# Odd token classes of the backward transforms as 256-point products, with the remaining rotation on VectorE and ScalarE, and x1's gradient added in a DMA

## The chip, the cores and the metric

One core of a Trainium2 chip runs the whole program in one launch. The metric is the device time of one execution in microseconds (us). The kernel before took 1410.86 us (median of 3 runs, 1408.94 to 1412.46).

## What is computed

A transformer-like block and its gradients. x is 2048 tokens by 1024 channels, F = 3584 hidden channels, all in bf16. Forward: a layer norm, scaled and shifted by rows made from `silu(c) @ w_mod`; a spectral filter; a second layer norm; a two-layer perceptron.

```python
X = rfft2(x); X = X * (w_r + 1j * w_i); y = irfft2(X)
...
h = _layernorm(x) * (1 + ca) + sa
x = x + ga * _A_ref(h, A_w_r, A_w_i)
h = _layernorm(x) * (1 + cb) + sb
x = x + gb * _B_ref(h, B_w1, B_b1, B_w2, B_b2)
```

The outputs are this result and its gradients with respect to x, the filter (w_r, w_i), both weights and biases of the perceptron, c and w_mod.

## The kernel before

The transforms are written as matrix products with cosine and sine matrices. Each input is first folded along channels and along tokens into sums and differences, which sorts the frequencies into four classes: CE and SE (cosine and sine at even token frequencies) and CO and SO (odd ones). Of the even classes a product needs only two of four blocks of 128 folded tokens for each output half; of the odd classes it needs all four.

`spectral_core` holds the stages, once forward (`fwd` true) and once for the backward pass. `s_fwd` transforms tokens of one class: eight blocks `c8` of 128 channels, each into one accumulator of 512 columns, by two products of 256 columns a half for an even class and four of 512 for an odd one (L531, L538); an evacuation copies it into `U`. Eight `pair` steps follow: a channel transform (L577), evacuation by ScalarE (L781), the product with the filter and the filter's gradient on VectorE, and the result in `R`. `beside_bwd` puts four fills and some steps of w_mod's gradient (`rows34`) beside each pair. After pair 5, `s_inv` transforms CE and SE back (L647), after pair 7 `s_inv_half` does CO and SO (L663), in the backward pass in two halves of 256 columns each. `V` then goes through the channel inverse (`po`, L749) into four chunks of tokens.

`consume_bwd` treats each chunk on VectorE: unfold (`unfold_d`, `unfold_tok`), a product (`tt(tmp, o4, n1, ALU.mult)`; every `tt` shows as L194) whose column sum on TensorE is `accCA` (`halves_sum`), the layer norm's backward (`ln_bwd`), the gradient of x1 loaded from `d_gx1` by the SP queue into the buffer `n1` and added, and the store: one plain DMA on SP and two indirect ones on POOL.

TensorE's other work is a list of pieces of 16 products (`pieces`): gradients of w2 (`gw2_product`), which need transposed tiles of hh, and then of w1 (`gw1acc`), whose results go through a ring of eight tiles to POOL's queue. `fill(n)` takes the next n of them, and the calls of `fill` by hand set where they stand between the stages. The pieces that are left run at the end.

Before the transforms, a loop over four blocks `b` of 512 tokens runs the perceptron's backward product (`pg_pass`, L1105), the two layer norms' backward on VectorE, and the fold of the block before (`fold_quarter` into `fbuf2`); column sums go to `acc3`. The `turn` there is a transposing copy and not part of the change.

Each engine runs its queue in order. The order is made when the program is built: a planner goes by the order in the program, a few raised priorities (`tc.high_priority`), explicit edges (`issue_after`, `behind`), and estimated costs and due times, so an instruction that it holds ready can stand ahead of one that comes earlier in the program. `nc.any` copies go to VectorE or ScalarE, as it chooses.

## Time and profile before

| | |
|---|---|
| median of 3 runs | 1410.86 us (1408.94 to 1412.46) |
| profiled execution | 1412.42 us |
| its span, first to last instruction | 1410.6 us |
| TensorE (PE) busy | 1374.2 us, 97% |
| VectorE (DVE) busy | 1072.4 us, 76% |
| ScalarE (ACT) busy | 739.2 us, 52% |
| GpSimd (POOL) busy | 351.2 us, 25% |
| mean granted TensorE clock | 0.992 |

A timeline row gives the start and the length in us from the span's start, the engine, the line, the operation, what it writes and reads with shapes, and how many instructions were merged; the bracket at its end is the idle time before it and who ended it. A group's row gives its count, busy time and mean ns of one. Matmuls are pipelined, so one lasts longer than the distance to the next: costs are read from start to start.

### The profile page before, as it was taken

The page shows a single profiled execution, that of the slowest core. Times are in us where ns is not written, and L with a number is a line of the kernel's source. Part 1 is how long each engine was busy: PE and PEld are TensorE (multiplying, and loading weights), DVE is VectorE, ACT ScalarE, POOL GpSimd, SP SyncE. Part 2 cuts the span into 40 slices and gives each one's busy share as a digit, 9 for nine tenths or more (in the row PEclk, how much of TensorE's full clock was granted, in tenths as well). Part 3 has the DMA queues.
Part 4 walks back from the last instruction along what each step waited for, and adds up shares of the span by engine and source line. Part 5 has one row for each costly group of instructions (what it writes and reads, how often), then busy time and mean ns, then how long its engine had stood idle before and what let it go on. Part 6 is the DMA issues. An engine that isn't in the chain of part 4 may idle for free. (4 is left out here: it accounts for less than half of the span.)

```text
span 1410.6 us, 18696 instructions
## 1 busy us (share of the span) xinstructions
PE 1374.2 (97%) x6963; PEld 664.5 (47%) x6963; DVE 1072.4 (76%) x1507; ACT 739.2 (52%) x1059; POOL 351.2 (25%) x436
## 2 busy tenths in 40 slices
PE   5998999999999999999999999999999999999999
PEld 2545565444444444444444444444544565444444
DVE  5897889987978777887620688999498757979960
ACT  4774667667877765665314583243622444434311
POOL 5510623201112122112210010112345330322341
PEclk8899999999999999999999999999999999999999
DMA  9972666899787777696999499996689996897971
GB/s 330 301 234 57 176 165 200 265 283 350 256 258 242 229 242 249 189 287 224 298 271 232 138 237 321 259 259 209 197 265 288 261 253 173 218 250 189 286 270 38
DMA packets 361265, 333.22 MB, mean 236 GB/s; under 512 B 208026, under 2 KB 303152, under 8 KB 361046
## 3 DMA queue, kind: packets, MB, share of 16 engines
q1 hardware_dynamic: 319990, 206.01, 55.9%
q0 software_dynamic: 35424, 120.78, 24.5%
q10 hardware_dynamic: 5760, 5.25, 1.2%
q8 instruction: 54, 0.88, 0.3%
q14 instruction: 37, 0.30, 0.1%
HBM read 166.77 MB, written 115.92 MB: 200 GB/s over the span
## 5 line engine op out<-in xcount | busy, mean ns | idle before, releaser
L1105 PE MATMUL pg<-w1T,gzr 128*128 128x512 bf16 x896 | 196.0, 379 | 2.8 <-ACT gn3b L1121 2.8
L814 PE MATMUL pp<-gBoT,wt 128*128 128x512 bf16 x896 | 197.9, 380 | 0.8 <-DVE phr L820 0.4
L1464 PE MATMUL gw1acc<-gzh,n3n 128*128 128x512 bf16 x640 | 140.0, 379 | 0.2 <-DVE gwo L1468 0.2
L1105 PEld LDWEIGHTS <-gzr 128*128 128x128 bf16 x896 | 86.6, 98 | 111.1 <-issue 8.5
L1464 PEld LDWEIGHTS <-n3n 128*128 128x128 bf16 x896 | 87.3, 98 | 107.1 <-issue 3.3
L951 PEld LDWEIGHTS <-w 128*128 128x128 bf16 x896 | 87.2, 98 | 107.0 <-issue 2.5
L814 PEld LDWEIGHTS <-wt 128*128 128x128 bf16 x896 | 87.5, 98 | 104.0 <-issue 1.5
L951 PE MATMUL pz<-n3Tb,w 128*128 128x512 bf16 x448 | 99.2, 379 | 1.0 <-DVE w2sD L1027 1.0
L951 PE MATMUL pz<-n3Ta,w 128*128 128x512 bf16 x448 | 98.7, 379 | 0.0
L1005 PEld LDWEIGHTS <-hhA 128*128 128x128 bf16 x608 | 59.0, 98 | 73.1 <-issue 2.8
L1239 PE MATMUL gw2acc<-gB,hhsA 128*128 128x512 bf16 x416 | 92.2, 379 | 0.0
L954 ACT ACTIVATE gt<-pz,b_col 128x512 bf16<-128x512 f32 x112 | 72.8, 683 | 33.2 <-PE pz L951 33.0
L962 ACT ACTIVATE gt<-gt 128x2048 bf16<-128x2048 bf16 x28 | 53.5, 1911 | 64.8 <-DVE gt L194 64.8
L194 DVE TENSOR_TENSOR gt<-gt,gt 128x2048 bf16<-128x2048 bf16 x56 | 68.6, 1224 | 19.8 <-ACT gt L964 18.5
L194 DVE TENSOR_TENSOR ct<-ct 128x2048 bf16<-128x2048 bf16 x68 | 80.6, 1218 | 0.9
L1468 ACT CAST gwo<-gw1acc 128x512 bf16<-128x512 f32 x50 | 28.4, 581 | 89.3 <-PE gw1acc L1464 78.5
L1247 ACT CAST gwo<-gw2acc 128x512 bf16<-128x512 f32 x40 | 23.3, 584 | 93.6 <-PE gw2acc L1239 90.5
L1239 PEld LDWEIGHTS <-hhsA 128*128 128x128 bf16 x416 | 40.7, 98 | 47.4
L1470 POOL DMA_DIRECT2D out_dram<-gwo x53 | 29.2, 554 | 129.8 <-DVE gwo L1468 67.6
L1464 PE MATMUL gw1acc<-gzu,n3n 128*128 128x512 bf16 x256 | 55.6, 379 | 1.2 <-ACT gwo L1468 1.2
L958 ACT ACTIVATE gt<-gt 128x2048 bf16<-128x2048 bf16 x28 | 53.5, 1909 | 2.1 <-DVE hhC L194 1.3
L964 ACT ACTIVATE gt<-gt 128x2048 bf16<-128x2048 bf16 x28 | 53.4, 1907 | 0.4
(347 smaller groups left out, 2558.4 us busy)
## 6 DMA issues: line engine op xcount, KB each, us to landing
gzr<-d_gz SPq DMA_DIRECT2D x28, 512.0 KB
wblk<-in_w_mod_dram SPq DMA_DIRECT2D x12, 1024.0 KB
out_dram<-otl POOLq DMA_DIRECT2D x48, 256.0 KB, 4.9
d_ph<-pho POOLq DMA_DIRECT2D x21, 512.0 KB, 6.0
d_hh<-hhA POOLq DMA_DIRECT2D x19, 512.0 KB, 5.1
w<-in_B_w_dram SPq DMA_DIRECT2D x7, 1024.0 KB
hhC<-d_ph SPq DMA_DIRECT2D x14, 512.0 KB
w2sA<-d_ph SPq DMA_DIRECT2D x14, 512.0 KB
```

The lines of the kernel that those rows point to most:

```text
L194: return nc.vector.tensor_tensor(out=out, in0=a, in1=b, op=op)
L814: last_pe[0] = nc.tensor.matmul(pp[:], lhsT=wt[:, fc % 4, cch, :], rhs=gBoT[j][:, cch, :], start=(cch == 0), stop=(cch == NDC - 1))
L951: last_pe[0] = nc.tensor.matmul(pz[:], lhsT=w1s[g][:, cch, k * P:(k + 1) * P], rhs=n3T[:, cch, :], start=(cch == 0), stop=(cch == NDC - 1))
L954: z_in = nc.scalar.activation(out=zb[:, k, :], in_=pz[:], func=ACT.Identity, bias=b1_col[:, fc:fc + 1], scale=1.0)
L958: nc.scalar.activation(out=av, in_=zb, func=ACT.Square)
L962: nc.scalar.activation(out=sg, in_=bv, func=ACT.Sigmoid, scale=2.0 * GK)
L964: nc.scalar.activation(out=bv, in_=bv, func=ACT.Sigmoid, scale=-2.0 * GK)
L1005: last_pe[0] = nc.tensor.matmul(pbs[i][:], lhsT=hh[:, k, i * P:(i + 1) * P], rhs=wp[:, k, :], start=False, stop=(g == 6 and k == 3))
L1105: last_pg[0] = nc.tensor.matmul(pgs[i][:], lhsT=gzs[b, g][:, k, i * P:(i + 1) * P], rhs=w1Ts[g][:, k, h * KH:(h + 1) * KH], start=(g == 0 ...
L1239: nc.tensor.matmul(acc[:], lhsT=hh_of(fc)[:, t, :], rhs=gBs[t // 4][:, t % 4, h * KH:(h + 1) * KH], start=(t == 0), stop=(t == NT - 1))
L1464: nc.tensor.matmul(acc[:], lhsT=n3ns[t // 4][:, t % 4, cch * P:(cch + 1) * P], rhs=gz2[t // 8][:, t % 8, :], start=(t == 0), stop=(t == NT ...
L1470: eng.dma_start(out=out_4[cch * P:(cch + 1) * P, fg * 512:(fg + 1) * 512], in_=ob)
```

## The change

The four blocks of an odd class come in two couples of mirrored rows. Each couple is rotated by an angle that depends only on the row (`al`: its sine, cosine, tangent, and two of them negated; one number per partition), in the form a + t b and b - t a, with the cosine moved into the matrix. After that an odd class needs products with 256 columns only, two of two blocks for each output half; the two halves `ab` are evacuated, and their sum and difference, written to every second column, are the class.

- `turn_tokens` rotates the folded tokens: for each couple four scalings by ScalarE and two sums by VectorE, for couple 0 in the loop at `b == 2`, for couple 1 after the last fold. `turn_R` does the same to `R` before the inverse, for couple 0 after pair 5 and for couple 1 after pair 7.
- `half_class` takes the place of `s_fwd` and of `s_inv_half` for CO and SO in the backward pass. `make_fm` builds its matrix from the small matrix `em2` by VectorE, after the ten fills ahead of the transforms; the load of `em2` moves ahead of them.
- The odd matrices are no longer stored to `d_SF` and loaded again.
- The scratch of `turn_R` and the evacuation buffer `ab` lie in the same part of `smbf`.
- The gradient of x1 is added to the chunk by an accumulating DMA from POOL's queue, in place of the SP load and a VectorE addition.
- Fills move: one ahead of each of CO and SO and two less beside pair 0; one between CO's and SO's inverse; 3, 7, 7, 8 instead of 4, 7, 6, 8 in the chunks, and one instead of two after the third chunk's column sum.

```diff
@@ spectral_core
         for cl in (CE, SE, CO, SO):
-            Us[cl] = s_fwd(cl, fb, sms[cl % 2][:, cl // 2], evac_u)
+            if fwd or cl % 2 == 0:
+                Us[cl] = s_fwd(cl, fb, sms[cl % 2][:, cl // 2], evac_u)
+            else:
+                Us[cl] = reg.tile([P, 8, 512], BF16, name=f"U{cl}", tag=f"uv{cl}")
+                fill(1)
+                half_class(cl, Us[cl], lambda c8, i, cl=cl: fb[:, i, cl, c8 * P:(c8 + 1) * P], evac_u)
...
+                if not fwd and par == 1 and m % 2 == 1:
+                    turn_R(R, m // 2)
                 beside(par * 4 + m, r_in[0])
...
         for cl in (CO, SO):
-            for hf in range(1 if fwd else 2):
-                s_inv_half(cl, smis[1], hf)
+            if fwd:
+                s_inv_half(cl, smis[1], 0)
+                continue
...
+            half_class(cl, Vs[cl], r_cols, evac_v)
+            if cl == CO:
+                fill(1)
@@ token rotation
+    def turn_pair(a, b, r, cls, t1, t2):
+        for k, cl in enumerate(cls):
+            neg, pos = (3, 2) if cl == CO else (2, 3)
+            nc.scalar.activation(out=t1[:, k], in_=b[:, k], func=ACT.Identity, scale=al[:, neg, r:r + 1])
+            nc.scalar.activation(out=t2[:, k], in_=a[:, k], func=ACT.Identity, scale=al[:, pos, r:r + 1])
+        tt(a, a, t1, ALU.add)
+        return tt(b, b, t2, ALU.add)
...
             fold_quarter(b - 1, pru, gn3s[(b - 1) % 2][:])
+            if b == 2:
+                turn_tokens(0, gn3s[1][:])
...
             fold_quarter(b, ftmp, n3u[:])
+            fold2_in[b] = turn_tokens(1, n3u[:])
@@ matrix, products, rotation of R
+    def make_fm():
+        for r in range(2):
+            cos, ncos = al[:, 1, r:r + 1], al[:, 4, r:r + 1]
+            for k in range(2):
...
+    def half_class(cl, dst, lhs, evac):
+        k = cl // 2
+        for c0 in range(0, 8, 2):
+            k0 = c0 % 4
+            for c8 in range(c0, c0 + 2):
+                pu = (ps_f if c8 % 2 else ps_s)("pu")
+                for t in range(2):
+                    cols = slice(t * 256, (t + 1) * 256)
+                    for r in range(2):
+                        last_pu[0] = nc.tensor.matmul(pu[:, cols], lhsT=lhs(c8, 2 * r + (t + k) % 2), rhs=fm[:, r, k, t, :],
+                                                      start=(r == 0), stop=(r == 1))
+                with tc.high_priority():
+                    evac(ab[:, k0 + c8 - c0].rearrange("p t w -> p (t w)"), pu[:])
+            dv = dst[:, c0:c0 + 2, :].rearrange("p c (j e) -> p c j e", e=2)
+            for e, op in ((0, ALU.add), (1, ALU.subtract)):
+                tt(dv[:, :, :, e], ab[:, k0:k0 + 2, k, :], ab[:, k0:k0 + 2, 1 - k, :], op)
+
+    def turn_R(R, r):
+        t1, t2 = (smbf[:, 2048 + k * 2 * PW:2048 + (k + 1) * 2 * PW]...[:, :, :, 0:DF] for k in range(2))
+        for cl in (CO, SO):
+            turn_pair(R[:, cl * 4 + 2 * r:cl * 4 + 2 * r + 1, :, 0:DF], R[:, cl * 4 + 2 * r + 1:cl * 4 + 2 * r + 2, :, 0:DF],
+                      r, (cl,), t1, t2)
@@ consume_bwd
-        nc.sync.dma_start(out=n1, in_=chunk_rows(d_gx1, i))
-        tt(o4, o4, n1, ALU.add)
+        nc.gpsimd.dma_start(out=o4, in_=chunk_rows(d_gx1, i), accum_op=ALU.add)
         store_tok(out_1, o4, i)
-        fill((4, 7, 6, 8)[i])
+        fill((3, 7, 7, 8)[i])
         halves_sum(accCA[0], tmp, i == 0, i == 3)
-        fill(2)
+        fill(1 if i == 2 else 2)
@@ ahead of the transforms
-    for cl in (CE, SE, CO, SO):
-        nc.sync.dma_start(out=(smA2, smB2)[cl % 2][:, cl // 2], in_=d_SF[:, cl, 0:4 if cl % 2 else 2])
+    for cl in (CE, SE):
+        nc.sync.dma_start(out=smA2[:, cl // 2], in_=d_SF[:, cl])
     sums3(3, gn3s[1], pru)
+    nc.sync.dma_start(out=em2, in_=d_E[:, 0])
     fill(10)
-    nc.sync.dma_start(out=em2, in_=d_E[:, 0])
+    make_fm()
@@ beside_bwd
         for k in range(4):
-            fill(1)
+            fill(1 if n > 0 or k > 1 else 0)
```

More of the change, by code (lines that the diff above doesn't have):

```diff
@@ L104 @@
     gb_col = const.tile([P, NDC], FP32, name="gb_col")
+    al = const.tile([P, 5, 2], FP32, name="al")
     d_x1 = dram.tile([S, D], BF16, name="d_x1")
@@ L1128, with turn_tokens @@
     nc.vector.tensor_copy(out=u_rt[:], in_=u_bfc[:])
+    tt(al[:, 1, :], al[:, 1, :], al[:, 1, :], ALU.mult)
+    nc.vector.tensor_scalar(out=al[:, 1, :], in0=al[:, 1, :], scalar1=-2.0, scalar2=1.0, op0=ALU.mult, op1=ALU.add)
+    nc.vector.reciprocal(out=al[:, 3, :], in_=al[:, 1, :])
+    tt(al[:, 2, :], al[:, 0, :], al[:, 3, :], ALU.mult)
+    nc.vector.tensor_scalar(out=al[:, 3:5, :], in0=al[:, 2:0:-1, :], scalar1=-1.0, scalar2=None, op0=ALU.mult)
+    def turn_pair(a, b, r, cls, t1, t2):
[5 more added lines that the diff above has]
+        return tt(b, b, t2, ALU.add)
+    def turn_tokens(r, tmp):
+        return turn_pair(fbuf2[:, 2 * r, 1:4:2, :], fbuf2[:, 2 * r + 1, 1:4:2, :], r, (CO, SO), tmp[:, 0:2, :], tmp[:, 2:4, :])
     def gmod_steps(r, wrs, gws, gr):
@@ new lines, in half_class @@
+    def half_class(cl, dst, lhs, evac):
[4 more added lines that the diff above has]
+                pu = (ps_f if c8 % 2 else ps_s)("pu")
+                for t in range(2):
+                    cols = slice(t * 256, (t + 1) * 256)
[7 more added lines that the diff above has]
+                tt(dv[:, :, :, e], ab[:, k0:k0 + 2, k, :], ab[:, k0:k0 + 2, 1 - k, :], op)
@@ L1356 @@
+    def turn_R(R, r):
+        t1, t2 = (smbf[:, 2048 + k * 2 * PW:2048 + (k + 1) * 2 * PW].rearrange("p (o x w) -> p o x w", o=1, x=2)[:, :, :, 0:DF] for k in range(2))
+        for cl in (CO, SO):
+            turn_pair(R[:, cl * 4 + 2 * r:cl * 4 + 2 * r + 1, :, 0:DF], R[:, cl * 4 + 2 * r + 1:cl * 4 + 2 * r + 2, :, 0:DF],
+                      r, (cl,), t1, t2)
     empf = reg.tile([P, 2048 + 4 * PW], BF16, name="empf", tag="wt")
```

23 lines of the change are left out of this document (19 added, 4 removed).

## The prediction

> **What bounds the kernel now.** I read the busy shares first, then TensorE's waits from 850 us on, then TensorE's timeline through the backward transforms, then the timelines of VectorE and ScalarE beside it.
>
> The page's busy shares, the list of waits and the end of TensorE's timeline (start, length, line, operation, idle before):
>
> ```profile
> PE 1374.2 (97%) x6963; PEld 664.5 (47%) x6963; DVE 1072.4 (76%) x1507; ACT 739.2 (52%) x1059; POOL 351.2 (25%) x436
> PE pg L1105 <- ACT gn3b L1121: 2.8, 1, 2.8
> PE accCA L217 <- DVE ct L194: 1.6, 1, 1.6
> PE gw1acc L1464 <- ACT gwo L1468: 1.2, 1, 1.2
> ```
>
> ```profile
> 1327.47 51.96 PE L1464 MATMUL gw1acc<-gzu,n3n 128*128 128x512 bf16 x240 [1.20 <-ACT gwo L1468]
> 1379.27 27.79 PE L1464 MATMUL gw1acc<-gzh,n3n 128*128 128x512 bf16 x128
> ```
>
> TensorE is busy for 97% of the span and ends it: the last 80 us are its own product stream. From 850 us on it waits for little more than the three rows show, and two of them (2.8 and 1.6 us) hang on VectorE's pace. So the span shortens by what TensorE loses, less whatever new wait stands in its queue. The question is whether VectorE and ScalarE keep up.
>
> **TensorE's saving.**
>
> ```profile
> 1005.59 1.90 PE L531 MATMUL pu<-smB,fbuf 128*128 128x512 bf16 x8
> 1007.74 12.25 PE L531 MATMUL pu<-smB,fbuf 128*128 128x512 bf16 x56 [0.25 <-ACT U L781]
> 1019.83 1.91 PE L577 MATMUL pcs<-empf,U 128*128 128x256 bf16 x16
> ```
>
> ```profile
> 1052.70 13.98 PE L1239 MATMUL gw2acc<-gB,hhsA 128*128 128x512 bf16 x64
> 1066.51 1.91 PE L577 MATMUL pcs<-empf,U 128*128 128x256 bf16 x16
> ```
>
> ```profile
> 1113.19 7.26 PE L647 MATMUL pv<-smf,R 128*128 128x256 bf16 x64
> 1120.28 1.91 PE L577 MATMUL pcs<-empf,U 128*128 128x256 bf16 x16
> ...
> 1151.40 14.22 PE L663 MATMUL pv<-smB,R 128*128 128x256 bf16 x128
> 1165.46 1.91 PE L749 MATMUL po<-gm,V 128*128 128x256 bf16 x16
> ```
>
> Forward, the two odd classes take 64 products of 512 columns, from 1005.59 to 1019.83: 14.24 us, 0.25 of it a wait. Afterwards they are 64 products of 256 columns; the even inverse shows those: 64 from 1113.19 to 1120.28, 7.09 us. Saving 7.15. Inverse, 128 products of 256 columns run from 1151.40 to 1165.46, 14.06 us; 64 remain, 7.03. Saving 7.03. **Sum: 14.2 us.** The odd matrices' store to memory (POOL) and their two loads (SP) are gone, and the load of the small matrix moves up on SP, past the loads of hh that ten fills issue, to where those stood; I cost it at nothing, since SP has that room. The fill products (16 matmuls; 64 take from 1052.70 to 1066.51, so 3.45 us each) are the same in number: two go from pair 0 to CO and SO, one from the first tail chunk to between the inverse classes, and one within the third chunk ahead of its column sum.
>
> **Turning the token classes.** Each of two turns is four scalings by ScalarE (128x1024) and two VectorE sums (128x2048).
>
> ```profile
> L514 ACT ACTIVATE xt<-xt,stats 128x1024 bf16<-128x1024 bf16 x16 | 18.8, 1240 | 0.0
> L194 DVE TENSOR_TENSOR ct<-ct 128x2048 bf16<-128x2048 bf16 x32 | 37.8, 1223 | 0.7
> ```
>
> ```profile
> 990.48 2.48 DVE L194 TENSOR_TENSOR fbuf<-fbuf,gzr 128x2048 bf16<-128x2048 bf16 x2
> 1007.11 0.68 DVE L194 TENSOR_TENSOR rows<-acc3b,au 64x512 bf16<-64x512 f32 x1 [9.41 <-ACT au L232]
> ```
>
> ```profile
> 889.79 1.22 DVE L194 TENSOR_TENSOR fbuf<-fbuf,pru 128x2048 bf16<-128x2048 bf16 x1
> 903.74 2.29 DVE L194 TENSOR_TENSOR pru<-gn3a,n2u 128x4096 bf16<-128x4096 bf16 x1
> ```
>
> ```profile
> 908.27 1.04 PE L217 MATMUL acc3a<-pru,ones_bf 128*32 128x512 bf16 x8
> 918.30 7.07 PE L1105 MATMUL pg<-w1T,gzr 128*128 128x512 bf16 x32 [2.84 <-ACT gn3b L1121]
> ```
>
> That is 4 x 1.24 = 5.0 us of ScalarE and 2 x 1.22 = 2.4 of VectorE a turn. The second turn follows the fold that ends at 992.96; its sums and the small matrix build (12 VectorE scalings) fall into the 9.4 us in which VectorE has nothing until 1007.1, and the odd classes are first read near 1009. Cost nil; without that gap it would be the 2.4 us. The first turn falls behind the fold that ends near 891, where VectorE has no gap: the backward normalisation follows at once, its product at 903.74 feeds a column sum that starts at 908.27, 2.3 us after that product ends, and TensorE already waits 2.84 us for evacuations that stand in ScalarE's queue behind that same normalisation. Between minus 2.8 (another order puts the evacuations first) and plus 2.4, I take **plus 1.5**: nearer the upper end, since nothing is removed there.
>
> **Half-size products.** Per pair of column blocks ScalarE evacuates two tiles and VectorE writes a sum and a difference (512 elements each, every second output element): 32 VectorE operations in all.
>
> ```profile
> L194 DVE TENSOR_TENSOR Pt<-cs01b 128x1028 bf16<-128x1028 bf16 x16 | 10.4, 690 | 9.2 <-ACT cs01b L781 9.2
> 1113.87 7.94 ACT L781 CAST V<-pv 128x512 bf16<-128x512 f32 x16
> 1166.10 0.69 DVE L754 CAST eb<-po 128x512 bf16<-128x512 f32 x1 [12.29 <-PE po L749]
> ```
>
> No row shows a strided VectorE output. Two bounds: half the 1028-element sum, 0.35 us; or the 512-element cast of the last row, 0.69. I take 0.69, since it is the only row with 512 elements: 32 x 0.69 = 22 us, 5.5 a class. (The Trainium skill, "VectorE: DVE Perf Modes", section "Mode 2×_1P — pack two bf16 into one 32-bit read", wants step ±1 for two elements a cycle; a step of 2 would fall to one a cycle. It speaks against the change, and by it the sum is the 22 us too; no run here shows it yet.) ScalarE's evacuations pitch at 7.94/16 = 0.50 us against TensorE's 0.44 a block, so a class lags it by half a microsecond, and a 3.45 us fill follows each. The forward half lies where VectorE waits, the inverse half in the 12.3 us idle before 1166.10. Cost nil if each class has its fill behind it; without that cover, 5.5 - 3.5 = 2 us a class.
>
> **Turning R and reaching the inverse.** Per turn ScalarE scales four 1026-element tiles, VectorE adds four.
>
> ```profile
> L194 DVE TENSOR_TENSOR R<-qa 128x1026 bf16<-128x1026 bf16 x16 | 10.4, 694 | 0.2
> 1124.28 1.30 DVE L194 TENSOR_TENSOR Pt<-cs01b 128x1028 bf16<-128x1028 bf16 x2 [2.80 <-ACT cs01b L781]
> 1139.10 1.30 DVE L194 TENSOR_TENSOR Pt<-cs01b 128x1028 bf16<-128x1028 bf16 x2 [4.96 <-ACT cs01b L781]
> 1145.19 1.30 DVE L194 TENSOR_TENSOR R<-qa 128x1026 bf16<-128x1026 bf16 x2
> ```
>
> Pair 7's R ends at 1146.5, 4.9 us before TensorE reaches the inverse. Now CO must be scaled (2 x 1.24) and added (2 x 0.69): 3.9 us, just inside. But the scratch of the turns is the evacuation buffer of the half products: CO's first evacuation waits until SO's scalings are read too, 3.9 + 2.5 + 0.7 = 7.1 us after R, and TensorE, two accumulators deep in one pool, needs it at 4.9 + 4 x 0.44 = 6.7 us, finished (0.6 more): 1.0 us late. Moreover TensorE comes 7.2 us sooner, against a cushion of 2.80 + 4.96 = 7.8 us on VectorE, into which turn 0 (4 x 0.69 = 2.8) goes: 2.2 us more. Bounds 0 and 6 (two scalings and their sums wholly open, plus 2); I take **plus 2**.
>
> **x1's gradient by DMA.** The add of 128x4096 leaves VectorE four times, the SP load with it; POOL gets four issues.
>
> ```profile
> 1177.81 0.69 DVE L754 CAST ct<-po 128x512 bf16<-128x512 f32 x1 [0.62 <-PE po L749]
> 1178.60 9.55 DVE L194 TENSOR_TENSOR ct<-ct 128x2048 bf16<-128x2048 bf16 x8
> 1188.24 2.29 DVE L194 TENSOR_TENSOR ct<-ct,xt 128x4096 bf16<-128x4096 bf16 x1
> ...
> 1246.74 2.29 DVE L194 TENSOR_TENSOR ct<-ct,xt 128x4096 bf16<-128x4096 bf16 x1 [4.59 <-DMA xt<-d_gx]
> 1267.07 0.61 PE L217 MATMUL accCA<-ct,ones_bf 128*32 128x512 bf16 x8 [1.59 <-DVE ct L194]
> ```
>
> VectorE loses 4 x 2.29 = 9.2 us and a 4.59 us wait ahead of the third chunk, whose column sum is the one that TensorE waits 1.59 us for; with one more fill ahead of it, that wait goes: **minus 1.6**. In the first chunk a fill is taken away: the last products end near 1177.6, the product that feeds the sum ends at 1190.5, 12.9 us, and three fills give 10.4: 2.5 us open, unless other ready products go first (then 0). I take **plus 1.5**. On POOL the accumulating transfer waits for the normalisation; behind it stand the scatters of the same chunk, which now wait for its landing, then stores of the weight gradient and loads of x. On SP the plain store waits likewise, and behind it the loads of gz.
>
> **Sum.** -14.2 + 1.5 + 2.0 - 1.6 + 1.5 = -10.8 us. The profiled execution took 1412.42 us (span 1410.6), 1.6 above the median of 1410.86: 1401.6 for such an execution, **1400.1** beside that median.
>
> **Rivals.**
> - *No new waits* (1395): the planner's order finds other products for each gap; -14.2 - 1.6 = -15.8. For it: TensorE has fills ready nearly everywhere, and waits little today. Against: pair 7's chain is serial. Chance 0.13.
> - *VectorE takes it back* (1407.6): the 22 us of half products, 2 x 2.4 and 2 x 2.8 of turns, 32 in all, and the matrix build outweigh the 9.2 removed, and TensorE waits a second time for pair 7, the whole 6, and for the first two column sums, 2.5 each: -14.2 - 1.6 + 1.5 + 6 + 5 = -3.3, so 1407.6. Against: VectorE's 12.3 and 9.4 us gaps lie where the work goes. Also here: the loads of hh, which don't come sooner when TensorE does. Chance 0.17.
> - *POOL blocked, slower* (1430): the scatters already hold POOL until VectorE is done, and now until the accumulation lands:
>
> ```profile
> 1215.46 1.74 POOL L166 DMA_INDIRECT out_dram<-ct,xu  x1 [2.75 <-DVE ct L194]
> out_dram<-gwo POOLq DMA_DIRECT2D x2, 128.0 KB, 2.5
> ```
>
>   The weight-gradient stores behind them don't leave, and the ring of 8 output tiles fills: 8 x 3.45 = 27.6 us of cover, less the 2.5 us of a store's own landing, 25; each microsecond of landing beyond that stops TensorE in each of three chunks. At 35 us it costs 30, less the 10.8: +19, 1430. It decides (slower) from a landing of 30. Against: the plain load that it replaces held VectorE for 4.59 us only. Chance 0.10.
> - *The change doesn't do what it says*: the products' count and shape are in the diff; I give it nothing.
>
> **How the numbers follow.** The forecast (1396 to 1405) has 0.60. A measurement here can tell 0.3%, 4.2 us: below 1406.6 counts as faster. Faster: 0.60 + 0.13, and 0.02 of the second rival, whose middle lies 1 us above that line: 0.75; same: the rest of it, 0.15; slower 0.10. The range runs from no new waits with today's 2.8 gone too (1410.86 - 14.2 - 1.6 - 2.8), 1392, to the second rival with loads late by one fill (3.45), 1411.
>
> **What would show it.** The odd forward stage of 64 products near 7 us in two parts with a fill each; 64 instead of 128 in the inverse; strided sums at 0.69 us; a wait of TensorE at the odd inverse on ScalarE or VectorE of 1 to 3 us; none at the third column sum. Wrong it is if TensorE's waits after 1000 us sum to over 10 us, if ScalarE waits for stores in the last stage, or if the stretch before 1000 us grows by over 3 us.

## The result, and the profile after

The changed kernel takes **1457.38 us** (median of 6 runs, 1453.53 to 1458.98), the kernel before 1409.97 (6 runs, 1407.46 to 1412.46): a ratio of **1.0332** (95% interval 1.0315 to 1.035). It is slower by 47 us where 10.8 less were forecast. The profiled execution took 1455.77 us, with a span of 1454.0; the span of before was 1410.6.

TensorE's busy time, from the page of the changed kernel:

```profile
PE 1373.4 (94%) x6899; PEld 661.2 (45%) x6899; DVE 1095.8 (75%) x1566; ACT 754.0 (52%) x1075; POOL 378.5 (26%) x438
```

64 matmuls are gone, and 64 others are half as wide: 14.2 us of work. But the busy time fell by 0.8 only (1374.2 to 1373.4), and the idle time rose from 36.4 to 80.6 us. The rest of the saved time went into slower products: the mean granted clock fell from 0.992 to 0.981. It is 0.93 from the first product of the backward transforms to the even inverse and 0.87 from there to the odd inverse, the two stages with the long waits; before has 1.00 in both. The view of waits of the changed kernel, TensorE's from 880 us on (total, times, longest):

```profile
PE pv L651 <- ACT V L803: 12.5, 1, 12.5
PE pu L1420 <- ACT smbf L803: 10.2, 7, 7.3
PE gw2acc L1277 <- DMA otl<-d_hhT: 9.1, 1, 9.1
PE gw2acc L1277 <- DMA hhsA<-d_hhT: 4.0, 2, 3.7
PE gw1acc L1540 <- DVE gwo L1544: 3.2, 2, 1.8
PE pg L1127 <- ACT gn3a L1143: 2.8, 1, 2.8
PE gw2acc L1277 <- DMA hhsA<-d_hh: 2.4, 1, 2.4
PE gw2acc L1277 <- DVE gB L195: 2.3, 1, 2.3
PE accCA L218 <- DVE ct L195: 0.7, 1, 0.7
```

The three waits of before were 2.8, 1.6 and 1.2. To see where they lie, I cut TensorE's timeline at four points: the first product of class CE of the backward transform (CE), of the even inverse, of the odd inverse, and of the output (`po`). The first cut, from TensorE's timeline of the kernel before and then of the changed kernel:

```profile
997.80 2.46 PE L538 MATMUL pu<-smf,fbuf 128*128 128x256 bf16 x21
```

```profile
1005.03 2.24 PE L542 MATMUL pu<-smf,fbuf 128*128 128x256 bf16 x19
```

The same cuts for every run that follows, in us (one profiled execution each; ratio with its interval from the timed runs, against the kernel before on the same chip):

| kernel | to CE | CE to even inverse | to odd inverse | to `po` | to the end | ratio |
|---|---|---|---|---|---|---|
| before | 997.8 | 115.4 | 38.2 | 14.1 | 245.1 | 1 |
| **after** | 1005.0 | **139.9** | **53.3** | 12.4 | 243.4 | 1.0332 (1.0315 to 1.0350) |
| plain_rows | 1004.1 | 124.1 | 51.1 | 11.8 | 243.3 | 1.0212 (1.0188 to 1.0237) |
| fills_back | 1007.7 | 133.6 | 52.9 | 11.2 | 249.0 | 1.0284 (1.0247 to 1.0320) |
| row5_late | 1003.8 | 115.5 | 53.4 | 12.2 | 243.4 | 1.0150 (1.0114 to 1.0187) |
| turnr_late | 1009.5 | 141.4 | 38.2 | 16.4 | 243.7 | 1.0238 (1.0214 to 1.0262) |
| turn0_late | 1004.5 | 142.4 | 53.2 | 13.9 | 243.4 | 1.0346 (1.0310 to 1.0383) |
| no_acc | 1006.1 | 141.6 | 52.5 | 12.3 | 239.5 | 1.0314 (1.0286 to 1.0341) |
| before_with_acc | 1000.0 | 115.4 | 38.2 | 15.2 | 258.6 | 1.0037 (1.0025 to 1.0049) |
| inv_only | 1000.2 | 115.4 | 49.4 | 11.3 | 243.6 | 1.0080 (1.0055 to 1.0105) |
| inv_only_r | 1005.1 | 115.4 | 38.2 | 14.2 | 243.8 | 1.0026 (1.0007 to 1.0044) |
| inverse_half_plain | 1001.8 | 115.4 | 38.2 | 14.3 | 245.0 | 1.0016 (1.0003 to 1.0029) |
| inverse_half_hold | 1006.5 | 115.4 | 38.2 | 13.5 | 238.6 | 1.0018 (1.0006 to 1.0030) |
| inverse_half_best | 1001.8 | 115.9 | 41.7 | 18.3 | 241.6 | 1.0036 (1.0020 to 1.0053) |
| two_later | 1006.1 | 118.2 | 38.2 | 14.7 | 243.5 | 1.0063 (1.0041 to 1.0085) |
| four_later | 1001.0 | 108.9 | 46.2 | 14.5 | 243.5 | 1.0048 (1.0033 to 1.0062) |
| both_halves_best | 1002.3 | 120.9 | 41.7 | 13.3 | 241.3 | 1.0055 (1.0039 to 1.0071) |
| all_later | 1003.6 | 108.5 | 44.7 | 23.2 | 243.5 | 1.0097 (1.0076 to 1.0118) |

Read the first column with care: the seven kernels that are alike up to CE with after (itself, plain_rows, fills_back, row5_late, turnr_late, no_acc, two_later) have 1003.8 to 1009.5 there, though their engines run the same instructions in the same order, but for a few neighbours that change places; and the two that are like before have 997.8 and 1000.0. In the other columns 115.4 and 38.2 come back to the tenth.

The loss of 43.4 us in the span is thus +7.2, **+24.5, +15.1**, -1.7 and -1.7. Four theories followed from the waits:

- **Theory 1**: between CE and the even inverse POOL's indirect transfers are starved by VectorE; SP waits for them, the loads of hh and w_mod come late, and TensorE waits (9.1, 4.0 and 2.4 us).
- **Theory 2**: in the odd forward classes the half-size sums stand in VectorE's queue behind steps for row 5 of w_mod's gradient, which wait for their loads; so ScalarE can't evacuate and TensorE waits (7.3 and less).
- **Theory 3**: the first turn of R (`turn_R(R, 0)`) stands in ScalarE's queue ahead of the even inverse's evacuations and waits for pair 5 (12.5).
- **Theory 4**: the first token turn in block 2 holds up evacuations and normalisation (2.8 and 2.3, and the clock).

The rivals: the accumulating DMA blocks POOL; or VectorE and ScalarE simply have too much to do.

### The profile page after: what moved, and what is told of

It reads as the page before. It is cut to its first block, busy times and chain, and to the rows that moved or that the text cites. A ratio compares the mean times of both kernels' runs of the same rounds, so it can differ in the third digit from the quotient of the medians.

```text
span 1454.0 us, 18659 instructions
## 1 busy us (share of the span) xinstructions
PE 1373.4 (94%) x6899; PEld 661.2 (45%) x6899; DVE 1095.8 (75%) x1566; ACT 754.0 (52%) x1075; POOL 378.5 (26%) x438
## 5 line engine op out<-in xcount | busy, mean ns | idle before, releaser
L1127 PEld LDWEIGHTS <-gzr 128*128 128x128 bf16 x896 | 87.0, 98 | 112.5 <-issue 10.8
L1540 PEld LDWEIGHTS <-n3n 128*128 128x128 bf16 x896 | 87.4, 98 | 108.9 <-issue 5.2
L1277 PE MATMUL gw2acc<-gB,hhsA 128*128 128x512 bf16 x416 | 95.6, 387 | 6.5 <-DMA hhsA<-d_hhT 4.0
L984 ACT ACTIVATE gt<-gt 128x2048 bf16<-128x2048 bf16 x28 | 53.5, 1911 | 64.5 <-DVE gt L195 64.5
L1285 ACT CAST gwo<-gw2acc 128x512 bf16<-128x512 f32 x40 | 23.2, 584 | 95.8 <-PE gw2acc L1277 48.2
L1197 DVE CUSTOM_DVE_ANT_0 otl<-otl 128x1024 bf16<-128x1024 bf16 x24 | 29.0, 1218 | 43.0 <-DMA otl<-in_w_mod_dram 38.7
L1277 PE MATMUL gw2acc<-gB,otl 128*128 128x512 bf16 x224 | 51.5, 386 | 9.1 <-DMA otl<-d_hhT 9.1
L980 ACT ACTIVATE gt<-gt 128x2048 bf16<-128x2048 bf16 x28 | 53.5, 1909 | 2.3 <-DVE hhC L195 1.6
```

What stands on the lines that cost most here:

```text
L980: nc.scalar.activation(out=av, in_=zb, func=ACT.Square)
L984: nc.scalar.activation(out=sg, in_=bv, func=ACT.Sigmoid, scale=2.0 * GK)
L1127: last_pg[0] = nc.tensor.matmul(pgs[i][:], lhsT=gzs[b, g][:, k, i * P:(i + 1) * P], rhs=w1Ts[g][:, k, h * KH:(h + 1) * KH], start=(g == 0 ...
L1197: step_in.append(nc.vector.tensor_tensor_reduce(out=buf, in0=buf, in1=gr, scale=1.0, scalar=0.0, op0=ALU.mult, op1=ALU.add, accum_out=gu[: ...
L1277: nc.tensor.matmul(acc[:], lhsT=hh_of(fc)[:, t, :], rhs=gBs[t // 4][:, t % 4, h * KH:(h + 1) * KH], start=(t == 0), stop=(t == NT - 1))
L1540: nc.tensor.matmul(acc[:], lhsT=n3ns[t // 4][:, t % 4, cch * P:(cch + 1) * P], rhs=gz2[t // 8][:, t % 8, :], start=(t == 0), stop=(t == NT ...
```

## Experiments: POOL's transfers (theory 1)

POOL's timeline of the changed kernel (start, duration, and in brackets the idle time before with its releaser), where VectorE runs without a pause from 1043.1 to 1078.95:

```profile
1048.96 5.04 POOL L562 DMA_INDIRECT ws<-in_A_w_r_dram,xu  x1 [0.30 <-issue]
1053.99 0.56 POOL L561 DMA_DIRECT2D ws<-in_A_w_i_dram  x1
1054.85 10.89 POOL L562 DMA_INDIRECT ws<-in_A_w_i_dram,xu  x1 [0.30 <-issue]
1066.05 13.77 POOL L635 DMA_INDIRECT out_dram<-empf,xu  x1 [0.30 <-DVE smf L195]
1080.13 0.99 POOL L635 DMA_INDIRECT out_dram<-empf,xu  x1 [0.30 <-issue]
```

Three indirect transfers take 5 to 14 us; the plain one between them takes 0.56. A gather and a scatter in POOL's timeline of the kernel before:

```profile
1058.31 2.02 POOL L558 DMA_INDIRECT ws<-in_A_w_r_dram,xu  x1 [0.30 <-issue]
...
1064.14 1.19 POOL L631 DMA_INDIRECT out_dram<-pf,xu  x1 [1.90 <-DVE pf L194]
```

turnr_late, turn0_late and no_acc have the same three long transfers (5.03 to 5.04, 10.88 and 13.78 us): it isn't a stray of one execution. In the changed kernel SP then waits for the scatter of `empf` before it can load into it, and everything behind it on SP comes late. From the waits of SP's queue in the changed kernel (total, times, longest):

```profile
SPq L565 <- DMA out_dram<-empf,xu: 23.6, 1, 23.6
```

**plain_rows** (the mirrored rows of pairs 0 to 3 by plain transfers in ascending order, so that their mirrored order is left out; the edit is shortened):

```
-                nc.gpsimd.indirect_dma_start(out=ws[:, x, 1 - sl, 0:DF], out_offset=None, in_=w, in_offset=w_idx(par, m))
+                if fwd or n > 3: (as before)
+                else: nc.gpsimd.dma_start(out=ws[:, x, 1 - sl, 0:DF], in_=w_up(w, m))   # and so for the scatters
```

> The changed kernel, but in pairs 0 to 3 the gathers of w and the scatters of w's gradient for the mirrored rows are plain transfers of 128 rows in ascending order on the same POOL queue (the mirrored order of those rows is left out). Work and order of VectorE, ScalarE, TensorE and SP stay as they are. Theory 1 (POOL's indirect transfers are starved while VectorE runs without a gap, and SP, then hh, w_mod and TensorE wait for the scatter): POOL's transfers take about 0.6 us each, SP's 23.6 us wait goes, with it TensorE's 9.1, 3.7 and 2.4 us, and most of the 12.5 us before the even inverse, since pair 5 is no longer late: 1425 to 1442 us. Rival (VectorE simply has too much to do in these stages): no change, 1454 to 1460 us.

Measured: ratio 1.0212, 17 us less. POOL's timeline of this run, beside the same stretch of VectorE (35.84 us, from 1039.4):

```profile
1044.97 0.54 POOL L569 DMA_DIRECT2D ws<-in_A_w_r_dram  x1
...
1052.76 1.14 POOL L647 DMA_DIRECT2D out_dram<-empf  x2 [6.12 <-DVE empf L199]
...
1067.82 8.33 POOL L567 DMA_INDIRECT ws<-in_A_w_r_dram,xu  x1 [0.31 <-issue]
```

And TensorE's timeline of the same run, at the even inverse:

```profile
1141.16 4.01 PE L662 MATMUL pv<-smf,R 128*128 128x256 bf16 x19 [11.04 <-ACT V L814]
```

Only the kind of transfer and the rows that it takes changed, and the stretch to the even inverse fell from 139.9 to 124.1: **15.8 us are POOL's**. The first transfer that was left indirect starves at once (8.33). The other part of the expectation failed: the wait in the even inverse stayed (11.0), so it doesn't hang on this.

**fills_back**

```
-                fill(1)
                 half_class(cl, Us[cl], ...)
-            fill(1 if n > 0 or k > 1 else 0)
+            fill(1)
```

> The changed kernel with its fills where they stood before: none ahead of CO and SO, four beside pair 0. Theory 1: pair 1 reaches VectorE 7 us later, gaps open between the pairs, the scatter leaves sooner: 10 to 20 us less there, against 2 us a class of cover lost in the odd classes: 1441 to 1451 us. Rival (VectorE has too much to do): only the lost cover shows, 1459 to 1463 us.

Measured: 1.0284, 6.8 us less, between the two expectations; its interval just touches that of the change. One scatter still took 10.95 us, until VectorE paused; the stretch to the even inverse fell by 6.3, and the tail was 5.6 us longer (TensorE waited 7.09 there on `gwo`). So the place of the fills is a part of it, and pausing VectorE by pacing pair 1 is not a cure.

**pool_beside_vector** and **pool_beside_vector_2** measure the disputed mechanism by itself; nothing of the kernel is computed in them.

> Not the kernel but a measurement beside it: eleven stages, in each of which POOL issues seven indirect gathers and one plain load of 128 rows while VectorE runs one kind of operation without a gap for 25 to 50 us (none; products of 2052 elements; the same with a pause after each; with a pause after every fourth; scaling by a constant; products of 1024; products with a running sum; copies with step 2; copies on one partition; sums of 512 with step 2 at the output; sums of 512 with step 1). Theory 1: a gather takes 1 to 2 us where VectorE idles or pauses after each operation, and 5 to 14 us beside products without a pause; the plain load 0.6 us in all stages. Rival (the queue's transfers were slow for another reason): 1 to 2 us in all stages. For the half-size sums: about 0.65 us at step 2, and half of that at step 1 if the step halves the rate.

> A second measurement beside the kernel: seven gathers and one plain load on POOL in each of eight stages. VectorE: nothing; 30 products of 2052 elements each on the result of the last; 32 that don't depend on one another; the same with a scaling by a constant after every fourth; four rounds of a pair's sums and products in the kernel's order with nothing to wait for; then nothing, the independent products, and the pairs again with eight loads of 1 MB on SP's queue beside them. Theory 1 in its narrower form (POOL gets in only where one VectorE instruction waits for another, and in the first measurement each waited for the one before): 1 to 2 us in the first two stages, 4 us and more for single gathers beside the independent products, shorter again with the scalings. Second form (it takes the loads of the other queues as well): long gathers only in the last two stages. Rival (neither; something else in the kernel holds POOL): below 2.5 us throughout.

In the first, no gather took longer than 1.96 us, beside any kind of VectorE work: theory 1 in its first wording (a stretch without a gap is enough) was wrong. In its products each needs the result of the one before; the sums in its last two stages don't, and there the longest gather took 1.44. POOL's timeline of the second:

```profile
97.52 1.97 POOL L268 DMA_INDIRECT gx<-in_A_w_r_dram,xu  x1 [0.30 <-issue]
...
104.05 0.59 POOL L266 DMA_DIRECT2D gx<-in_A_w_r_dram  x1
...
132.06 39.70 POOL L268 DMA_INDIRECT gx<-in_A_w_r_dram,xu  x1 [21.18 <-DVE bx L311]
...
183.83 1.97 POOL L268 DMA_INDIRECT gx<-in_A_w_r_dram,xu  x1 [0.30 <-issue]
...
285.56 35.76 POOL L268 DMA_INDIRECT gx<-in_A_w_r_dram,xu  x1 [44.17 <-DVE fx L313]
```

Rows 1 and 2, a gather and the plain load, lie beside independent products, row 3 beside the same with a scaling after every fourth: one gather takes 39.70 us, the whole stage, and no other transfer runs meanwhile (0 GB/s). Row 4 lies beside the pairs' order, row 5 beside the same order with loads on SP: again the whole stage, 35.76, and the loads had ended (0 GB/s) for the last 11 us of it. So VectorE alone can hold a gather for as long as it runs without a pause; but in stages that look alike the gather gets in within 1.97 us. Which of the two happens isn't settled by these runs: row 3 differs from row 1 by the scalings and row 5 from row 4 by the loads, one reading for each. The stage with loads and independent products doesn't help: its gathers (0.95) had ended at 241.4, before VectorE began at 248.7. The Trainium skill ("SBUF — State Buffer", section "Who interferes with whom") says that a VectorE instruction with two SBUF inputs contends with GpSimd instructions that read SBUF, and, of VectorE's two-port modes, that whoever issues first has the shared ports for the whole instruction. That the gathers, which read their row numbers (`xu`) from SBUF, are held and the plain load between them in the kernel isn't (0.56) agrees with the first. That one wait spans some forty instructions is more than the page says. It also infers that `tensor_tensor` doesn't stall the making of descriptors. Row 2 agrees for the plain load; the indirect one was held for the last 11 us of row 5 beside products and sums alone.

## Experiments: orders of queues (theories 2, 3, 4)

Beside the odd forward classes VectorE has an idle stretch in the kernel before; it ends on a load of w_mod, for a step of row 5:

```profile
1020.84 1.23 DVE L1159 CUSTOM_DVE_ANT_0 otl<-otl 128x1024 bf16<-128x1024 bf16 x1 [7.29 <-DMA otl<-in_w_mod_dram]
```

VectorE's timeline in the odd forward classes of the changed kernel:

```profile
1023.12 3.91 DVE L195 TENSOR_TENSOR U<-smbf 128x512 bf16<-128x512 bf16 x6
1030.26 1.23 DVE L1197 CUSTOM_DVE_ANT_0 otl<-otl 128x1024 bf16<-128x1024 bf16 x1 [3.23 <-DMA otl<-in_w_mod_dram]
1031.40 0.08 DVE L1197 DVE_READ_ACCUMULATOR2_ANT gu<- 128x1 f32 x1
1032.74 1.23 DVE L1197 CUSTOM_DVE_ANT_0 otl<-otl 128x1024 bf16<-128x1024 bf16 x1 [1.26 <-DMA otl<-in_w_mod_dram]
...
1034.69 4.51 DVE L195 TENSOR_TENSOR U<-smbf 128x512 bf16<-128x512 bf16 x7
```

The sums are 0.65 us apiece as forecast, but between the seventh (one stands ahead of these rows) and the eighth lie 7.7 us: two steps for row 5, each waiting for its load. Three more such steps stand ahead of the first sum. The buffer of four evacuated blocks is full, so ScalarE stops, so TensorE does (TensorE's timeline of the changed kernel):

```profile
1036.14 1.01 PE L1420 MATMUL pu<-smbf,fbuf 128*128 128x256 bf16 x4 [7.28 <-ACT smbf L803]
```

**row5_late**

```
+                if cl == SO:
+                    for step in step_in[3:8]:
+                        behind(step, last_cmb[0])      # the last sum of SO
```

> The changed kernel, but the last five steps for row 5 of w_mod's gradient are issued behind the last sum of SO instead of among the sums of CO and SO. Theory 2 (these steps wait for their transfers and hold the sums behind them, and so the evacuations, in the odd forward classes): TensorE's waits of 7.3 and 1.2 us there go, and the stretch from CE to the even inverse falls by 5 to 9 us, if the five steps (8.5 us of VectorE) don't prolong the stretch without gaps; by theory 1 they do, and part comes back: 1448 to 1458 us. Rival (the strided sums themselves are too slow for the class): the waits on ScalarE there stay above 5 us.

Measured: 1.0150, 25 us less, below the expected range (1448 to 1458 us). TensorE's timeline of row5_late:

```profile
1015.02 3.66 PE L1425 MATMUL pu<-smbf,fbuf 128*128 128x256 bf16 x32
1018.52 3.62 PE L1280 MATMUL gw2acc<-gB,otl 128*128 128x512 bf16 x16
1021.97 3.66 PE L1425 MATMUL pu<-smbf,fbuf 128*128 128x256 bf16 x32
...
1110.82 8.66 PE L1280 MATMUL gw2acc<-gB,hhsA 128*128 128x512 bf16 x32 [5.03 <-DMA hhsA<-d_hh]
```

Two classes of 3.5 us with a fill between, and no wait: just what the prediction had drawn. And the pairs lose nothing to POOL: its indirect transfers take 1.2 to 2.0 us, though VectorE runs without a gap for 36.6 us from 1049.7 on, longer than in the changed kernel. So a run without a gap isn't enough to hold them. The two losses have one root in this kernel, the five steps' place: they make VectorE late for the pairs, and in that phase POOL starves. 115.5 us are back to the time of before, not 7 below it: the loads of hh don't come sooner (5.03), as the prediction's second rival had said.

**turnr_late** starts from these rows of ScalarE's timeline of the changed kernel:

```profile
1153.06 1.15 ACT L1160 ACTIVATE smbf<-R,al 128x1026 bf16<-128x1026 bf16 x1 [11.31 <-DVE R L195]
...
1157.21 1.15 ACT L1161 ACTIVATE smbf<-R,al 128x1026 bf16<-128x1026 bf16 x1 [0.66 <-DMA out_dram<-gwo]
1158.27 0.56 ACT L1285 CAST gwo<-gw2acc 128x512 bf16<-128x512 f32 x1
1158.73 3.12 ACT L803 CAST V<-pv 128x512 bf16<-128x512 f32 x6
```

```
-                if not fwd and par == 1 and m % 2 == 1:
-                    turn_R(R, m // 2)
+                if not fwd and par == 1 and m >= 2:
+                    with tc.issue_after(last_v[0].ins):    # last evacuation of the even inverse
+                        turn_R(R, m - 2)
```

> The changed kernel, but the first turn of R (8 scalings and sums) is issued behind the evacuations of the even inverse. Theory 3 (its scalings stand in ScalarE's queue ahead of those evacuations and wait for pair 5): TensorE's 12.5 us wait in the even inverse goes, 1443 to 1447 us. Rival (pair 5 is late by itself and the wait only moves to pair 6 or 7 or to the odd inverse): 1454 to 1460 us.

Measured: 1.0238, 13 us less. The wait of 12.5 is gone and the stretch is 38.2, that of before; 4.0 come back in the odd inverse (16.4 for 12.4), whose waits (1.97 and less) now show both turns, in TensorE's timeline of turnr_late:

```profile
1150.88 7.26 PE L651 MATMUL pv<-smf,R 128*128 128x256 bf16 x64
...
1191.07 1.59 PE L1422 MATMUL pu<-smbf,R 128*128 128x256 bf16 x13 [1.42 <-DVE R L195]
1194.63 2.01 PE L1422 MATMUL pu<-smbf,R 128*128 128x256 bf16 x16 [1.97 <-ACT smbf L805]
```

Theory 3 stands, and it is independent of theory 1 (inv_only, below, shows the same wait with pair 5 on time).

**turn0_late**

```
-            if b == 2:
-                turn_tokens(0, gn3s[1][:])
...
+            turn_tokens(0, ftmp)
             fold2_in[b] = turn_tokens(1, n3u[:])
```

> The changed kernel, but the first token turn (scalings of 128x1024 and two sums of 128x2048) is done behind the last fold, beside the second, not in block 2. Theory 4 (in block 2 it holds up evacuations, normalisation and the stores behind them): TensorE's waits of 2.8 and 2.3 us before the transforms go and the forward classes start 7 us sooner, 1449 to 1452 us. Rival (the turn has to be paid somewhere: the odd forward classes wait for it instead): 1455 to 1460 us.

Measured: 1.0346, no gain (after: 1.0332). The waits of 2.8 and 2.3 went, one of 3.37 on the evacuations of `gn3b` came, which the kernel before has too (2.84). CE starts at 1004.5, within the spread of its kind, and the odd classes wait 2.95 and 5.24 instead of 1.19 and 7.28. Theory 4 isn't borne out as a loss that can be moved away; the turn is paid in either place.

**two_later** (row5_late and turnr_late together) and **four_later** (with turn0_late, and with `(0, 1, 2, 3, 3, 3, 2, 3)` for `(1, 2, 2, 3, 3, 3, 0, 3)` in `beside_bwd`):

> The changed kernel with two steps moved in the order: the last five steps of row 5 behind the last sum of SO, and the first turn of R behind the evacuations of the even inverse. If theories 2 and 3 name separate losses, they add up: ratio 1.015 less the 11 us (15 in the even inverse, 4 given back in the odd) that the late turn brought by itself, 1.005 to 1.008 of the kernel before. Rival (VectorE, delayed by the five steps, is then late for the odd inverse): 1.012 or more.

> The run above, with the first token turn behind the last fold as well, and the steps for rows 3 and 4 spread over the pairs as 0, 1, 2, 3, 3, 3, 2, 3 instead of 1, 2, 2, 3, 3, 3, 0, 3. If the 5.0 us wait for a transposing load of hh comes from SP standing behind loads of w_mod, it goes; the first turn gives back 2 to 5 us: 0.997 to 1.002 of the kernel before. Rival (the transfers of hh themselves come no sooner): that wait stays at 4 us or more, 1.003 to 1.006.

Measured: 1.0063, as expected, and 1.0048, the rival's time, though its wait didn't stay. The two losses add up: two orders take back 38 of the 47 us, with all of the change's work still there; so it isn't the amount of VectorE's and ScalarE's work that cost them. In four_later the wait for hh goes and the stretch from CE is 108.9, **6.5 us below before: the forward half's saving**, at last. But 8.0 us are lost right behind it (46.2 for 38.2): TensorE waits 5.44 in the even inverse on ScalarE, which stands idle for 8.7 us ahead of an evacuation of `gwo`. This order has two steps beside pair 6 that stood beside pairs 0 and 1; that they are the cause is likely but not shown.

## Experiments: the accumulating DMA

**before_with_acc** is the kernel before with the four lines of `consume_bwd` changed, the transfer and the tail's fills together; **no_acc** the changed kernel with them undone.

> The kernel before, with nothing but the accumulating DMA in place of load and sum, and the tail's fills as in the change. By the prediction the third column sum's 1.6 us wait goes and the first gets up to 1.5: 0.998 to 1.001 of the kernel before. Rival (the accumulating transfer holds POOL, the stores of the weight gradient and with them TensorE): 1.004 or more, with waits of TensorE on gwo above 4 us.

> The changed kernel with the load and the sum of x1's gradient back in place of the accumulating DMA, and the fills of the tail as before. If the accumulating DMA costs here what it costs the kernel before (5 us), 1.028 to 1.031 of the kernel before, against the change's 1.033. If the tail of the changed kernel hides it (its waits on gwo were 1.4 and 1.8 us in the profile): 1.032 to 1.035.

Measured: 1.0037, 5 us slower than before; and 1.0314, against 1.0332 for the change, whose intervals overlap, so that no gain is shown there. The profiled execution of before_with_acc (1429.18 us, well over its median of 1419.18) shows the first half of the mechanism of the prediction's third rival. TensorE's, POOL's and VectorE's timelines of before_with_acc, in this order:

```profile
1272.53 12.87 PE L1463 MATMUL gw1acc<-gzh,n3n 128*128 128x512 bf16 x48 [13.06 <-DVE gwo L1467]
```

```profile
1240.47 1.40 POOL L1390 DMA_DIRECT2D ct<-d_gx  x1
...
1259.89 1.02 POOL L166 DMA_INDIRECT out_dram<-ct,xu  x1 [17.42 <-DMA ct<-d_gx]
```

```profile
1270.65 1.23 DVE L194 TENSOR_TENSOR ct<-eb 128x2048 bf16<-128x2048 bf16 x1 [21.81 <-DMA out_dram<-ct]
```

POOL waits 17.42 us for the landing, the store of the chunk leaves that much later, VectorE waits 21.81 us to write the next chunk into the same buffer, and an evacuation of `gwo` queues behind it in VectorE's queue; TensorE goes on as it ends (1272.5). The rival had the stop come from the ring of eight output tiles instead. In after the same wait of POOL is 8.07 us, and TensorE waits 1.4 and 1.8. So the four lines cost the kernel before a few us, more in some executions; the transfer without the moved fills wasn't run.

## Experiments: what each half is worth

**inv_only** undoes the forward half (512-column products, no token turns, fills as before, the small matrix built beside pair 1); **inv_only_r** moves the turn as in turnr_late besides.

> The changed kernel with the forward half of the change undone: the odd forward classes are 64 products of 512 columns again, no token turns, the fills where they stood before; the inverse half (turns of R, 64 products of 256 columns) and the accumulating DMA stay, and the small matrix is built beside pair 1. Theories 1, 2 and 4 put their losses (15.8 us in the pairs, about 9 us in the odd classes, some us in block 2) on the forward half, so all three go, and the inverse half shows what it is worth: if pair 5 is on time again, little is left of the 12.5 us wait, and 1402 to 1410 us come out, faster than the kernel before. Rival (turning R costs VectorE and ScalarE that much by itself, whatever happened ahead of it): the wait in the even inverse stays at 8 to 12 us, 1412 to 1420 us.

> The run above, with the first turn of R issued behind the evacuations of the even inverse. Theory 3: no wait in the even inverse at all, up to 4 us of waits in the odd inverse instead (as the late turn showed there), 1402 to 1408 us. Rival (both turns then stand between pair 6 and the odd inverse and VectorE is late for it): 1408 to 1416 us.

Measured: 1.0080, above both expectations, and 1.0026, the rival's time. CE to the even inverse is 115.4 in both, so the 24.5 us belong to the forward half. In inv_only the wait of theory 3 stays (9.08 us), as its rival said: pair 5 is on time and the scalings still come too late.

Five attempts at a version that keeps its saving, all without the accumulating DMA: **inverse_half_plain** (inv_only_r without it), **inverse_half_hold** (the last three steps of rows 3 and 4 behind the odd inverse's last sum), **inverse_half_best** (a further fill ahead of the odd inverse), and for both halves **both_halves_best** and **all_later** (row steps spread as `(0, 1, 2, 2, 2, 3, 4, 3)`).

> The inverse half of the change alone: forward half undone, no accumulating DMA, the first turn of R behind the even inverse, and one more fill taken from the end to stand ahead of the odd inverse, where the second turn made TensorE wait. By the terms measured so far: 1.0026, less 0.0037 for the DMA, less 2 to 4 us of cover: 0.995 to 0.998 of the kernel before. Rival (the cover only moves the wait on, or the tail misses the fill): 0.999 to 1.002.

> Both halves of the change, without the accumulating DMA, with the first token turn behind the last fold, the five steps of row 5 behind SO, the first turn of R behind the even inverse, and the additional fill ahead of the odd inverse. Both halves' products would give 14 us; what the loads of hh, VectorE and ScalarE take back of the forward half's 7 decides: 0.995 to 0.998 if half of it stays, 0.998 to 1.002 if nothing does (then the inverse half alone is the better version).

> The inverse half without the accumulating DMA and without the additional fill: only the first turn of R moved. 1.0026 of the run with the DMA less the 0.0037 that the DMA cost the kernel before: 0.998 to 1.000. Rival (the two don't add, the tail hides the DMA): 1.002 to 1.004.

> The run above, with the last three steps for rows 3 and 4 issued behind the last sum of the odd inverse instead of between the turn of R and those sums. If VectorE's queue there is the rest of the loss (two such steps, 2.4 us, stood ahead of the turn's last sums, and TensorE waited 1.8 us): 2 to 4 us less than the run above, 0.995 to 0.998. Rival (ScalarE's queue with its stores decides): no change against the run above.

> Both halves with every loss found taken away by order alone: no accumulating DMA, the first token turn behind the last fold, row 5's last five steps behind SO, the first turn of R behind the even inverse, rows 3 and 4 spread as 0, 1, 2, 2, 2, 3, 4, 3 with the last three steps behind the odd inverse. From CE to the end the forward half gave 6.5 us in one run (four_later) and the inverse half 7.1 in another (inverse_half_hold); if both hold together, 400 to 403 us there instead of 412.8, and with the 2 to 4 us that the stretch ahead of CE has lost in these versions 0.995 to 0.998 of the kernel before. Rival (the same engines can't hide both at once): 0.999 to 1.004.

Measured: 1.0036, 1.0055, 1.0016, 1.0018, 1.0097. **None beats the kernel before**, and none comes as low as its first expectation. Yet one execution of inverse_half_hold takes 405.7 us from CE to the end, where before takes 412.8. These 7.1 us aren't simply the products' 7: without the fill that moved between the classes (3.45) the odd inverse saves 4.0, and small waits and gaps take the other 3; the tail saves 3.1, as the waits of before there (1.6 and 1.2) don't occur. The largest wait in TensorE's timeline of inverse_half_hold, at the odd inverse:

```profile
1162.83 2.01 PE L1425 MATMUL pu<-smbf,R 128*128 128x256 bf16 x16 [0.81 <-ACT smbf L808]
```

What it gains is lost ahead of CE (1006.5). The five kernels without the forward half have 1000.2 to 1006.5 there in the same order of instructions, so a part of that is chance; but in all five TensorE waits 3.2 to 3.5 us at `pz`, where before has 1.0. I name no cause for that; the angles' few instructions are all that these kernels add there. In the medians inverse_half_hold gains nothing on inverse_half_plain (1.0018 and 1.0016). In all_later the row steps, moved to pair 6 and behind the odd inverse, go with a VectorE that is late for R (4.83 us at the odd inverse), and what the stretch from CE had won as in four_later (108.5, 6.9 less than before) is given back twice over (44.7 for 38.2 and 23.2 for 14.1). inverse_half_best had its additional fill's store stand in ScalarE's queue ahead of the evacuations that it was to cover.

## Why the prediction was wrong

The result lies far outside 1392 to 1411, on the side that had a chance of 0.10, and not by that case's mechanism. By the steps of the prediction:

- **TensorE's saving, 14.2**: the products take about what was said (7.0 us forward in row5_late; 7.8 in the inverse of inv_only, 0.4 of it a wait). Right as work; as time it was used up by idle time and by slower products after it.
- **First token turn, 1.5**: the stretch ahead of CE grew by 7.2 in the trace, against a bar of 3 that the prediction had set; the waits that it names explain about 3 of it (2.8 and 2.3 for 2.84, and a column sum that is no longer hidden), slower products some more, and kernels alike up to there differ by 5.7. Mis-sized, but small.
- **Second turn and matrix, nil**: nothing in the runs speaks against it.
- **Half-size sums, nil**: *this step failed*. The price was right (0.69 estimated, 0.65 measured). The cover was right too, as row5_late shows. What failed is "the forward half lies where VectorE waits": that gap (7.29 us in the row of before above) was where VectorE waited for loads of w_mod, for five steps that stand in its queue ahead of the sums and among them. A gap that ends on a load isn't free for work that is queued behind the waiter. It cost 24.5 us instead of 0, and all but 0.1 of that goes in row5_late, where only these steps stand elsewhere. 15.8 of it came by way of POOL's gathers and scatters beside a late VectorE, which the prediction had not weighed at all.
- **Turns of R, 2 (0 to 6)**: *failed by its first turn*. The prediction followed the second through pair 7 and gave the first only its four sums on VectorE, 2.8 us, against a cushion; its four scalings on ScalarE were not placed in the queue, where the evacuations of the even inverse follow. +15.1. The odd inverse itself, on which the 2 us were spent, had waits of 0.35, 0.58 and 0.20; it takes 12.4 us, where 64 products and the fill make 10.5, so that part was about right.
- **x1 by DMA, -1.6 and +1.5**: the third column sum's wait did go, the first has 0.7. But the four lines alone cost the kernel before 5 us, about a sixth of the third rival's 30: POOL waited for the landing as that rival had it, and TensorE was stopped by way of VectorE's queue, not by the ring.
- **Second rival, VectorE takes it back (1407.6)**: its last sentence, that the loads of hh don't come sooner, came true in row5_late (5.03 us).

The Trainium skill's rule cited there ("VectorE: DVE Perf Modes", section "Mode 2×_1P — pack two bf16 into one 32-bit read") is borne out by pool_beside_vector, whose groups of instructions by line (busy, mean ns of one) show sums of 512 elements with step 2 and with step 1 at the output:

```profile
L284 DVE TENSOR_TENSOR ax<-bx 128x512 bf16<-128x512 bf16 x40 | 29.3, 732 | 1.4
...
L285 DVE TENSOR_TENSOR ax<-bx 128x512 bf16<-128x512 bf16 x40 | 17.1, 427 | 1.4
```

It spoke against the change by 22 us of VectorE; that was not what lost the time.

## What to carry to other kernels

Ask of every gap into which you put work what ended it. If it was a load for an instruction that stands ahead in the same queue, the work waits too, and so does all that needs its buffer. For each instruction that a change adds, an engine's helpers included, write down its neighbours in the queue: two lines of order (five row steps, one turn) carried 38 of the 47 us. And when the cover of a stage goes, follow what the busier engine does to POOL's indirect transfers and to SP behind them; a saving on the bounding engine is worth nothing where the load behind it doesn't come sooner.

## What the hardware showed

- A POOL gather or scatter by row numbers, 0.95 us by itself, can be held through many VectorE instructions, at the longest until VectorE pauses: 5.04, 10.89 and 13.77 us in the kernel, the same to 0.01 us in other executions of that order; 39.70 and 35.76 measured alone. Plain transfers take 0.5 to 0.6 beside VectorE. It doesn't happen always (1.97 beside like work, and 36.6 us without a gap in row5_late did no harm), and what decides was not found.
- TensorE's products are often slower after a long wait, so a wait can cost more than its length. TensorE's timeline of after:

```profile
891.80 11.12 PE L1127 MATMUL pg<-w1T,gzr 128*128 128x512 bf16 x44 [2.81 <-ACT gn3a L1143]
...
1159.37 7.86 PE L651 MATMUL pv<-smf,R 128*128 128x256 bf16 x48 [12.54 <-ACT V L803]
```

At the pace of undisturbed rows (7.07 us for 32 of 512 columns, 7.26 for 64 of 256) they would take 9.7 and 5.4: 1.4 and 2.4 us more. The granted clock was 0.64 in the first 4 us of the first row and 0.67 in the second. Not every wait does it: behind 2.84 us in the kernel before the clock was 1.00, and behind 2.41 us in after 32 products of 512 columns took 7.08.
- Kernels that are alike up to a point differ by 5.7 us there at 1005 us, so a few us ahead of a stage can't be read from one trace.
